# Two-operation wide factors with shifted phases, and seeds without a square root

## The chip, the cores and the metric

The kernel runs on one core of a Trainium2 chip. The metric is device time in microseconds of one execution; the kernel is one launch. Its engines run side by side, each with its own queue in program order: TensorE (PE, matmuls), VectorE (DVE), ScalarE (ACT, activation functions from loaded tables), GpSimd (POOL) and SyncE (SP, here only issuing transfers). They wait for each other with semaphores. PSUM is the memory that matmuls write to; SBUF is the large on-chip memory.

## The reference

A block with adaptive normalization around an S4 convolution, and a bilinear GLU. Shapes: u is 1x2048x640, the state has 192 entries for each of 640 channels, the GLU is 640 to 1536 and back, the modulation vector c has 640.

```python
mod = (silu(c) @ w_mod).reshape(1, 6, 1, 640)        # sa, ca, ga, sb, cb, gb
h = layernorm(x) * (1 + ca) + sa
x = x + ga * S4(h)
h = layernorm(x) * (1 + cb) + sb
x = x + gb * ((h @ w_gate) * (h @ w_up)) @ w_down

# S4: dt = exp(log_dt); A, B, C complex, 640 x 192
P = exp((dt * A)[:, :, None] * l)                    # l = 0 .. 2047
K = einsum("dn,dnl,dn->dl", C, P, dt * B).real       # the filter, 640 x 2048
y = irfft(rfft(pad(u)) * rfft(pad(K)))[:2048] + u * Dskip
```

## The kernel before, in words

The time falls into three parts: the startup and the filter with its Fourier transforms (to about 445 us), the rest of the convolution (to 546), and the GLU (to the end).

**The filter.** The sum over 192 states for 2048 positions is made as matmuls of two factors. A position is split into a low and a high part; for each of 40 blocks (n = 0 to 39, `NK`; eight for each of 5 groups, `db`, of 128 channels) the kernel builds four factor tiles: PtA and QtA (16 of 24 rows of the states), PtB and QtB (the other 8). P has 32 columns a row, Q, the wide factor, has 64. Each is a magnitude times a cosine and a sine. POOL makes the magnitudes EQ (128x1536) and EP (128x768) and the phases Ph (128x1536, 32-bit integers, where a whole turn is the whole range of the integer) by `outer` (L802) out of small tables: `tab_ph` (L785 to L787) makes LH from DL, and `tab_eq` (L796, L797) makes LQ from RL. ACT turns Ph into sines and cosines (`trig`, tiles tra and trb in PSUM, two buffers). DVE multiplies both (`qmul`, L857 to L859, for QtA and QtB; L864 for PtA, L884 for PtB), and PE multiplies the factors (L899, L914) into kg. EQ and EP have two buffers each, Ph two, QtA one.

**The seeds.** What a channel group starts from is made once per group by `u_seeds(db)`: from A, B, C and dt come rho (log magnitude), f (the frequency), and x and y, the real and imaginary part of B times C. From x and y the kernel needs a real amplitude and a phase: before, the modulus by two squares, an add and a square root, then the ratio of y to modulus and |x| added up, by a reciprocal and clipped to one, whose arctangent gives half the angle, psi; the amplitude is the modulus with x's sign. `trans` moves a 128x192 tile into the row order of the factors by matmuls against permutations (three matmuls a tile). RL and RH are multiples of rho (L681, L683), of which exponentials give RL, RH and LP. Each step is a letter, and the strings `SEG0` (first group) and `SEG` (groups 1 to 4) say which letters are issued together; a table of due times, which the change leaves alone, sets where a group of letters goes between the blocks. Seed 0 belongs to the startup; seeds 1 to 4 come at about 62 to 111, 157 to 197, 252 to 287 and 337 to 368 us. The scratch of these steps lies in three PSUM banks (psfa, psfb, psfc).

**The startup.** `mod_i` makes silu(c) into `sil` on ACT; `modrow` (L455) multiplies it with the six parts of w_mod, which are loaded through two tiles, t_tw and t_ti, one part after another; `u_fold` (L474 to L488) turns the rows into columns `mcol` and folds them into the factors' scale. The startup loop issues seed 0's letters and puts POOL's first tables between them at given positions (`P_PH`, `P_EP`, `P_MOD`).

**Order.** Every engine's order is the order in which the code issues the work. The loop over t (three steps per block) issues ACT's trig of a block, the seeds' and transforms' units that are due, DVE's products, POOL's tables for the next block and PE's matmuls. The names `ab`, `f16`, `gh`, `TV`, `Kta` in the rows are the Fourier transforms' and the normalization's tiles.

Of the kernel before, what the change touches and what calls it, by code (L numbers as in the profile page):

```python
# [18 lines left out]
P = 128  # L19
# [295 lines left out]
def tile_kernel(ctx: ExitStack, tc: tile.TileContext, I, out):  # L315
# [87 lines left out]
    V.memset(dskt, 0.0)  # L403
    xa = ring(f16, [P, 5, D], "f16")
# [179 lines left out]
    LP = [pk1.tile([P, 96, 8], F32, name=f"LP{i}") for i in range(3)]  # L584
    LH = pk1.tile([P, 192, 8], I32, name="LH")
    for t in LP:
        V.memset(t[:, :, 0:1], 1.0)
    RH = [pk1.tile([P, 11, 96], F32, name=f"RH{i}") for i in range(3)]
    RL = [pk1.tile([P, 4, 96], F32, name=f"RL{i}") for i in range(2)]
# [5 lines left out]
    def u_seeds(db):  # L595
# [7 lines left out]
        rho, f, amp = prm[:, 0, :], prm[:, 1, :], prm[:, 0, :]  # L603
        x, u, y, v = tb_[:, 0, :], tb_[:, 1, :], ta[:, 1, :], ta[:, 1, :]
# [3 lines left out]
        Rh, Rl, Dh, Dl, Lp = ([R[(2 * db + h) % len(R)] for h in range(2)] for R in (RH, RL, DH, DL, LP))  # L608
        g4 = lambda t: t.rearrange("p k (s r) -> p k s r", r=24)
# [7 lines left out]
        def trans(src, o):  # L617
            PE.matmul(o[:, :, 0:16], src[:, 0:128], perm[:, 0:128], start=True, stop=True)
            PE.matmul(o[0:64, :, 16:24], src[:, 128:192], perm[:, 128:192], start=True, stop=True)
            PE.matmul(o[64:128, :, 16:24], src[:, 128:192], perm[:, 192:256], start=True, stop=True)  # L620
# [32 lines left out]
        def s_c():  # L653
            ps = bank("ps").rearrange("p c (s r) -> p c s r", r=24)
            T["ps"] = ps
            trans(rho, ps[:, 0])
            trans(f, ps[:, 1])
            q = bank("q")
            act(u, x, AF.Square)
            act(q[:, 0], y, AF.Square)  # L660

        def s_d(h):
# [11 lines left out]
            if h:  # L674
# [3 lines left out]
        def s_r(h):  # L678
            ps = T["ps"]
            free(h, "ep", "eq", "lq")  # L680
            V.tensor_tensor(g4(Rl[h])[:, 0:3], ps[:, 0, hs[h]].unsqueeze(1).to_broadcast([P, 3, 4, 24]),  # L681
                            mults[:, 11:14].unsqueeze(2).unsqueeze(3).to_broadcast([P, 3, 4, 24]), op=OP.mult)
# [3 lines left out]
        def s_u():  # L686
            V.tensor_tensor(u, u, T["q"][:, 0], op=OP.add)
# [1076 lines left out]
```

## Time and profile before

| | |
|---|---|
| median of 3 runs | 995.83 us (995.24 to 996.85) |
| profiled execution, own time | 1000.16 us |
| its span in the profile | 998.3 us |
| mean granted TensorE clock | 0.955 |
| PE / DVE / ACT / POOL busy | 889.1 / 770.0 / 581.0 / 574.7 us |
| table loads on ACT | 24, 30.8 us in all |

A row of the timeline says when an instruction starts, how long it lasts, the engine, the line of the kernel, the operation, the tile written and the tiles read, the shape, how many such instructions the row stands for, and in brackets how long the engine was idle before it and which instruction released it. L320 is the helper of all activations on ACT. Rows of the chain of waits have a start, a length and what the time was spent on.

### The profile page before, as it was taken

Reading aid. Unit: us, or ns where it says so; the run is one execution under the profiler, and the core shown is the slowest. Engines: PE = TensorE matmul, PEld = TensorE weight load, DVE = VectorE, ACT = ScalarE, POOL = GpSimd, SP = SyncE. Lnnn points to the kernel's source line nnn. Section 1 sums busy time; section 2 is a strip of 40 time slices with the busy share of each in tenths; the row PEclk is TensorE's granted clock in tenths of the full one; section 3 lists DMA queues with packets and bytes.
Section 4 is the critical chain, followed back from the end, with each engine's and each line's share of the span. In section 5 each row is a group of like instructions: output and inputs, shape, how many; then the busy total and the mean of one; then the engine's idle time right before and its main releaser. Section 6 shows DMA issues by size and latency. Waiting matters only on the chain.

```text
span 998.3 us, 26784 instructions
## 1 busy us (share of the span) xinstructions
PE 889.1 (89%) x11190; PEld 728.2 (73%) x11190; DVE 770.0 (77%) x1391; ACT 581.0 (58%) x1055; POOL 574.7 (58%) x424
## 2 busy tenths in 40 slices
PE   4874699799889778997988999999999999999998
PEld 3653466576666466776766888879998888889998
DVE  8698568987989988795989877787576887768452
ACT  4759999987889797874574222235473422224331
POOL 4976899899869989960056667650112454442000
PEclk9867799899989989999999999999999999999999
DMA  7654665454545534559732542535635232212341
GB/s 243 239 145 155 217 237 163 159 165 135 154 131 161 171 108 149 161 152 305 221 113 59 188 169 69 184 132 159 211 133 202 96 98 80 79 53 63 96 159 53
DMA packets 141961, 148.96 MB, mean 149 GB/s; under 512 B 8976, under 2 KB 120080, under 8 KB 140432
## 3 DMA queue, kind: packets, MB, share of 16 engines
q1 hardware_dynamic: 140688, 146.33, 46.3%
q8 instruction: 88, 1.44, 0.6%
q10 hardware_dynamic: 1152, 0.92, 0.3%
q14 instruction: 33, 0.27, 0.1%
HBM read 108.36 MB, written 38.86 MB: 147 GB/s over the span
## 4 chain that ended last, share of the span: by engine, by line
PE 59%; ACT 14%; DVE 13%; issue 6%; POOL 5%; DMA 2%; DVEq 0%; SPq 0%; ACTq 0%; POOLq 0%
PE pa L1182 26%; PE pa L1597 16%; ACT tra L320 2%; ACT L320 2%; PE psfc L981 1%; ACT trb L320 1%; PE kg L899 1%; PE psfb L981 1%; PE psfa L1041 1%; PE kg L914 1%; POOL EQ L802 1%; PE psfb L1041 1%; PE psfa L981 1%; PE psfc L936 1%; POOL Pha L802 1%
## 5 line engine op out<-in xcount | busy, mean ns | idle before, releaser
L802 POOL TENSOR_TENSOR EQ<-LQ,RH 128x1536 f32<-128x1536 f32 x40 | 124.2, 3105 | 21.9 <-DVE QtB L859 21.7
L320 ACT ACTIVATE z<-pa 128x512 f32<-128x512 f32 x24 | 14.4, 599 | 166.4 <-PE pa L1182 115.4
L1146 DVE TENSOR_TENSOR wsgl<-wga,wsgh 128x640 fp32r<-128x640 f32 x72 | 68.2, 950 | 46.7 <-ACT wsgh L320 46.7
L320 ACT ACTIVATE wsgh<-wga 128x640 fp32r<-128x640 f32 x72 | 52.6, 732 | 71.2 <-PE pa L1597 39.8
L1546 POOL TENSOR_TENSOR z<-z,s 128x512 f32<-128x512 f32 x24 | 33.5, 1395 | 98.6 <-DVE s L1545 98.6
L1597 PE MATMUL pa<-wsgh,sh 128*128 128x384 f32 (+1 forms) x304 | 69.6, 310 | 0.0
L1597 PE MATMUL pa<-wsgl,sh 128*128 128x384 f32 (+1 forms) x304 | 69.3, 309 | 0.0
L1597 PE MATMUL pa<-wsgh,sl 128*128 128x384 f32 (+1 forms) x304 | 69.2, 309 | 0.0
L802 POOL TENSOR_TENSOR EP<-LP,RH 128x768 f32<-128x768 f32 x40 | 66.1, 1653 | 0.0
L1158 POOL TENSOR_TENSOR tf<-wur,wgb 128x256 f32<-128x256 f32 x24 | 19.2, 801 | 80.9 <-DVE wtl L1146 54.7
L802 POOL TENSOR_TENSOR Pha<-LH,DH 128x1536 int32<-128x1536 int32 (+1 forms) x21 | 62.5, 2974 | 3.0 <-ACT trb L320 2.6
L802 POOL TENSOR_TENSOR Phb<-LH,DH 128x1536 int32<-128x1536 int32 x20 | 62.3, 3117 | 2.9 <-ACT tra L320 2.9
L1146 DVE TENSOR_TENSOR wtl<-tf,wth 128x256 fp32r<-128x256 f32 (+1 forms) x72 | 60.0, 859 | 0.0
L914 PE MATMUL kg<-QtB,PtB 64*32 64x64 f32 x2560 | 47.9, 226 | 8.4 <-DVE QtB L858 8.4
L914 PEld LDWEIGHTS kg<-QtB,PtB 64*32 64x32 f32 x2560 | 40.9, 113 | 16.0 <-DVE QtB L858 9.5
L1544 DVE TENSOR_TENSOR s<-pa,s 128x512 f32<-128x512 f32 x24 | 16.6, 691 | 45.2 <-PE pa L1182 40.1
L1182 PE MATMUL pa<-sl,wth 128*128 128x512 f32 x144 | 45.2, 395 | 2.1 <-DVE sl L1146 2.1
L1597 PEld LDWEIGHTS pa<-wsgh,sl 128*128 128x128 f32 x304 | 46.6, 188 | 0.0
L1597 PEld LDWEIGHTS pa<-wsgl,sh 128*128 128x128 f32 x304 | 46.6, 188 | 0.0
L1597 PEld LDWEIGHTS pa<-wsgh,sh 128*128 128x128 f32 x304 | 46.5, 188 | 0.0
L1182 PE MATMUL pa<-sh,wth 128*128 128x512 f32 x144 | 45.1, 395 | 1.1 <-ACT sh L320 1.1
L1182 PE MATMUL pa<-sh,wtl 128*128 128x512 f32 x144 | 45.4, 397 | 0.0
(608 smaller groups left out, 2957.3 us busy)
## 6 DMA issues: line engine op xcount, KB each, us to landing
wga<-wdg SPq DMA_DIRECT2D x24, 640.0 KB, 4.0
wga<-B_w_gate SPq DMA_DIRECT2D x12, 640.0 KB, 5.7
wgb<-B_w_gate SPq DMA_DIRECT2D x24, 320.0 KB, 3.4
wur<-B_w_up SPq DMA_DIRECT2D x24, 320.0 KB, 4.0
xb<-x2d SPq DMA_DIRECT2D x6, 1280.0 KB, 7.4
TVb<-WD SPq DMA_DIRECT2D x22, 256.0 KB, 3.4
t_tw<-w_mod SPq DMA_DIRECT2D x3, 1600.0 KB, 7.8
t_ti<-w_mod SPq DMA_DIRECT2D x3, 1600.0 KB, 7.7
```

The lines of the kernel that those rows point to most:

```text
L320: return S.activation(o, i, f, **kw)
L802: G.tensor_tensor(o.rearrange("p x (h l) -> p x h l", l=8), lo.unsqueeze(2).to_broadcast([P, rows, nh, 8]), hi.rearrange("p h x -> p x h") ...
L899: PE.matmul(kg[j * 32 : j * 32 + 32, dd, :], PtA[:, c, dl * 4 + j, :], QtA[:, c, dl * 4 + j, :], start=dd == 0 and c == 0, stop=False, til ...
L914: PE.matmul(kg[j * 32 : j * 32 + 32, dd, :], PtB[lo : lo + 64, c, r, :], QtB[lo : lo + 64, c, r, :], start=False, stop=dd == 7 and c == 1, ...
L981: PE.matmul(r[c][par * 64 : par * 64 + 64, i, :], t_tw[:, k0 + k, c, :], src[:, k, :], start=True, stop=True, tile_position=(0, par * 64))
L1041: PE.matmul(r[par][:, i], w, v, start=c == 0, stop=c == 1, tile_position=(lo, 0))
L1146: V.tensor_tensor(lo, v, hi, op=OP.subtract)
L1158: G.tensor_tensor(t[:, 0:2], u[:, 0:2], g[:, 0:2], op=OP.subtract)
L1182: PE.matmul(ps, w[a][:, k], x[b][:, l], start=n == 0 and m == 0, stop=n == 2 and m == len(ks) - 1)
L1544: V.tensor_tensor(S67[i], ps, S6[i], op=OP.add)
L1546: G.tensor_tensor(ZT[i], ZT[i], S67[i], op=OP.add)
L1597: PE.matmul(ACC[tb][t][c], x[:, ts], w[:, cs], start=st, stop=f == NF - 1 and n == 2 and (c == 0 or t % 2 == 1))
```

## The change

Three things change together.

1. `qmul` makes a wide factor in two operations in place of three. The phases are put an eighth of a turn ahead (`eighth`, added where `tab_ph` copied DL into LH, and in psi), so that the sign that one third of a wide factor needed falls away; the two halves of the 64 columns then differ only in which of sine and cosine is read first.
2. The seeds have no Square, Abs and Sqrt. The step x makes q = x·y and its sign, prm = 2·(y, x)·sign, and adds and subtracts it; the step X takes reciprocal and quotient, clipped to one on both sides; f takes the arctangent, and a sine and a cosine of it; n adds a quarter turn by sign; m multiplies x and y with the cosine and sine, and G adds the two by accumulating both in the same matmul group. For groups 1 to 4, RL and RH of both halves come from one operation each (B), and so do the exponentials (E); LP, RH and RL are single tiles with the halves side by side.
3. In the startup a sine of a constant is issued first on ACT, the letters have a new order, and `mod_i` is issued with the first EP, at loop position 9, where it stood at position 1.

```diff
-SEG0 = ("l", "a", "b", "c", "ud", "r", "x", "e", "f", "G", "g", "D", "h", "v", "R", "")
-SEG = ("l", "a", "b", "c", "ud", "D", "r", "R", "x", "eE", "f", "g", "h", "v")
-P_PH, P_EP, P_MOD = 3, 6, 1
+SEG0 = ("l", "a", "b", "cx", "d", "X", "f", "nh", "vr", "e", "mG", "D", "", "", "R", "")
+SEG = ("l", "a", "b", "cx", "d", "D", "X", "B", "f", "E", "nm", "G", "h", "v")
+P_PH, P_PSI, P_EP = 3, 7, 9
...
-        def trans(src, o):
-            PE.matmul(o[:, :, 0:16], src[:, 0:128], perm[:, 0:128], start=True, stop=True)
...
+        def trans(o, *srcs):
+            for t, c, k in ((o[:, :, 0:16], slice(0, 128), 0), (o[0:64, :, 16:24], slice(128, 192), 128), (o[64:128, :, 16:24], slice(128, 192), 192)):
+                for i, src in enumerate(srcs):
+                    PE.matmul(t, src[:, c], perm[:, k : k + c.stop - c.start], start=i == 0, stop=i == len(srcs) - 1)
...
-            act(u, x, AF.Square)
-            act(q[:, 0], y, AF.Square)
+            bank("q")
...
-            act(u, u, AF.Sqrt)
-            act(pe[:, 0], x, AF.Abs)
-            V.tensor_scalar(pe[:, 1], x, 0.0, 0.5, op0=OP.is_ge, op1=OP.subtract)
...
+            q = T["q"][:, 0]
+            V.tensor_tensor(q, x, y, op=OP.mult)
+            V.tensor_scalar(sgn, q, 0.0, 0.5, op0=OP.is_ge, op1=OP.subtract)
+            V.scalar_tensor_tensor(prm, tb_[:, 1::-1, :], 2.0, sgn.unsqueeze(1).to_broadcast([P, 2, N]), op0=OP.mult, op1=OP.mult)
+            V.tensor_tensor(x, x, prm[:, 0, :], op=OP.add)
+            V.tensor_tensor(y, y, prm[:, 1, :], op=OP.subtract)
+
+        def s_X():
+            q = T["q"][:, 0]
+            V.reciprocal(q, x)
+            V.tensor_scalar(q, q, 3e38, -3e38, op0=OP.min, op1=OP.max)
+            V.tensor_tensor(q, y, q, op=OP.mult)
+            V.tensor_scalar(arg, q, 1.0, -1.0, op0=OP.min, op1=OP.max)
 
         def s_f():
-            pe = T["pe"]
+            T["pe"] = pe = bank("pe")
+            act(arg, arg, AF.Arctan)
+            act(pe[:, 1], arg, AF.Sin)
+            act(pe[:, 0], arg, AF.Sin, scale=-1.0, bias=halfpi)
+
+        def s_n():
+            V.scalar_tensor_tensor(arg, sgn, 0.5 * math.pi, arg, op0=OP.mult, op1=OP.add)
+
+        def s_m():
...
+            V.scalar_tensor_tensor(xy, xy, dt2[:, db : db + 1], T["pe"], op0=OP.mult, op1=OP.mult)
...
-        G.tensor_copy(lh[..., 0:1], one(d[0]))
-        G.tensor_tensor(lh[..., 1:2], one(d[0]), one(d[1]), op=OP.add)
...
+            G.tensor_tensor(lh[..., 0], d[0], eighth[:, a : a + 1].unsqueeze(2).to_broadcast([P, 4, 24]), op=OP.add)
+        G.tensor_tensor(lh[..., 1:2], lh[..., 0:1], one(d[1]), op=OP.add)
...
-        return [lambda: V.tensor_tensor(Qt[:, :, :, 0:32], tr[:, :, :, ::-1], e[:, :, 0:32].unsqueeze(1).to_broadcast([P, 2, R, 32]), op=OP.mult),
-                lambda: V.tensor_tensor(Qt[:, 0, :, 32:64], tr[:, 0], e[:, :, 32:64], op=OP.mult),
-                lambda: V.scalar_tensor_tensor(Qt[:, 1, :, 32:64], tr[:, 1], -1.0, e[:, :, 32:64], op0=OP.mult, op1=OP.mult)]
+        return [lambda h=h: V.tensor_tensor(Qt[:, :, :, 32 * h : 32 * h + 32], tr[:, ::-1] if h else tr[:, :, :, ::-1],
+                                            e[:, :, 32 * h : 32 * h + 32].unsqueeze(1).to_broadcast([P, 2, R, 32]), op=OP.mult) for h in range(2)]
...
+    act(colT[:, 0:1], halfpi, AF.Sin)
     exp_acc(dt, ldt)
...
-        elif i == P_EP:
+        elif i == P_PSI:
+            tab_ph(0, 0)
+            mk_ph(0, 0)
+        elif i == P_EP:
+            mod_i()
             mk_ep(0)
-        elif i == P_MOD:
-            mod_i()
-    tab_eq(0)
-    tab_ph(0, 0)
-    mk_ph(0, 0)
-    mk_eq(0)
+            tab_eq(0)
+            mk_eq(0)
```

What this does to the order of the instructions is seen at two places. The first is ACT's queue in the startup, where `sil` is the operand of the modulation matmuls, tra the transposed amplitude and LP, RH, RL the exponentials of half 0. Before:

```order
L320 ACTIVATE psfb<-ptb 128x2x192
L320 ACT_TABLE_LOAD
L320 ACTIVATE sil<-ccol 128x5
L320 ACTIVATE ptb<-ptb 128x192
L320 ACTIVATE psfa<-pta 128x192
L320 ACT_TABLE_LOAD
L320 ACTIVATE ptb<-ptb 128x192
L320 ACTIVATE psfb<-ptb 128x192
L320 ACT_TABLE_LOAD
L320 ACTIVATE LP_147<-RL_157 128x96 x7
```

Now:

```order
L320 ACTIVATE psfb<-ptb 128x2x192
L320 ACTIVATE pta<-pta 128x192
L320 ACTIVATE psfb<-pta 128x192
L320 ACTIVATE psfb<-pta,halfpi 128x192
L320 ACT_TABLE_LOAD
L320 ACTIVATE LP<-RL 128x96 x7
L320 ACTIVATE RH<-RH 128x1056
L320 ACTIVATE RL<-RL 128x288
L320 ACTIVATE RL<-tra 128x2x96
L320 ACT_TABLE_LOAD
L320 ACTIVATE sil<-ccol 128x5
```

The Silu has moved behind the arctangent, the exponentials and the copy of the amplitude. The second place is DVE's queue in seed 4, with the factors of the blocks around it. Before:

```order
L864 TENSOR_TENSOR PtAa<-tra,EP_144 128x1024
L884 TENSOR_TENSOR PtB<-trb,EP_144 128x512
L857 TENSOR_TENSOR QtB<-trb,EQ_142 128x16x32
L858 TENSOR_TENSOR QtB<-trb,EQ_142 128x8x32
L859 SCALAR_TENSOR_TENSOR QtB<-trb,EQ_142 128x8x32
L687 TENSOR_TENSOR ptb<-ptb,psfc 128x192
L667 CAST psfc<-psfa 128x192
```

Now (ptb, pta and prm are in SBUF, psfc in PSUM):

```order
L882 TENSOR_TENSOR PtAa<-tra,EP_147 128x1024
L703 TENSOR_TENSOR psfc<-ptb 128x192
L704 TENSOR_SCALAR pta<-psfc 128x192
L705 SCALAR_TENSOR_TENSOR prm<-ptb,pta 128x384
L706 TENSOR_TENSOR ptb<-ptb,prm 128x192
L707 TENSOR_TENSOR ptb<-ptb,prm 128x192
L902 TENSOR_TENSOR PtB<-trb,EP_147 128x512
L876 TENSOR_TENSOR QtB<-trb,EQ_145 128x16x32 x2
L679 CAST psfc<-psfa 128x192
```

The five operations of x now stand between the factors PtA and PtB of one block, where one add stood behind QtB. The chain that made the quotient, ten rows further down before, is the step X, and stands ahead of the joint RL and RH.

More of the change, by code (lines that the diff above doesn't have):

```diff
@@ L655, in s_c @@
             T["ps"] = ps
[L656 to L660 removed]
+            trans(ps[:, 0], rho)
+            trans(ps[:, 1], f)
+            bank("q")
         def s_d(h):
```

108 lines of the change are left out of this document (53 added, 55 removed).

## The prediction

> **What bounds the kernel now.** I read the stage windows first, then POOL's waits, then the chain of waits, and last the timeline of single engines where the chain changes hands. The windows show each engine's busy time by stage (us, busy PE, PEld, DVE, ACT, POOL, granted clock, DMA share, GB/s):
>
> ```profile
> 118.00:445.00 327.00, 284.11 (x6656) 211.70 (x6652) 277.83 (x464) 282.70 (x502) 298.61 (x174) 0.95 0.51 158
> ...
> 546.00:998.00 452.00, 445.19 (x2372) 394.67 (x2372) 312.70 (x504) 157.11 (x304) 164.16 (x151) 1.00 0.38 125
> ```
>
> From 546 us PE is busy 445.2 of 452 us, and nothing of the change lies there: what is lost or won earlier passes through to the end. From 118 to 445 us POOL is busiest (298.6 of 327, 28.4 us idle), with ACT and DVE 16 and 21 us behind it. Two of POOL's waits in the whole run (total, times, longest):
>
> ```profile
> POOL EQ L802 <- DVE QtB L859: 21.7, 7, 7.1
> ...
> POOL DL L742 <- issue: 9.7, 2, 8.1
> ```
>
> So POOL stops where DVE has not yet freed an EQ buffer, or where a seed's psi (made by L737 on DVE, used by L742) is late. A delay of DVE between two blocks is a delay of POOL once the two EQ buffers are used up. The chain of waits (start, length) before that stage is not POOL:
>
> ```profile
> 18.77 4.57 PE psfb L455 x10
> ...
> 27.05 6.77 DMA t_tw<-w_mod
> ...
> 39.57 1.03 PE kg L899 x64
> ```
>
> The modulation rows (L455) run first, the tile t_tw is loaded again behind them, and the first block's matmuls (L899) stand behind that in PE's queue.
>
> **The wide factors.** One block's QtA, start by start on DVE:
>
> ```profile
> 82.93 1.23 DVE L857 TENSOR_TENSOR QtA<-trb,EQ 128x1024 f32<-128x1024 f32 x1 [0.53 <-issue]
> 84.07 0.68 DVE L858 TENSOR_TENSOR QtA<-trb,EQ 128x512 f32<-128x512 f32 x1
> 84.67 0.68 DVE L859 SCALAR_TENSOR_TENSOR QtA<-trb,EQ 128x512 f32<-128x512 f32 x1
> 85.27 0.34 DVE L687 TENSOR_TENSOR ptb<-ptb,psfb 128x192 f32<-128x192 f32 x1
> ```
>
> 1.14 + 0.60 + 0.60 = 2.34 us become two of 1.14, 2.28 us. By the same step QtB saves as much at most, so 0.12 us a block, 4.8 us of DVE over 40 blocks, in a stage where DVE has 49 us of idle time. I count it only beside seed 4, with 0.4. The eighth of a turn costs POOL one add for a copy in a table, 0.1 us for each of ten tables; I set it to nothing.
>
> **Startup.** Before, the Silu that the modulation rows need is out early; ACT now does it last, behind the arctangent, the exponentials and the copy of G's result into RL:
>
> ```profile
> 8.03 0.21 ACT L320 ACTIVATE sil<-ccol 128x5 f32<-128x5 f32 x1
> 12.17 1.25 DVE L683 TENSOR_TENSOR RH<-psfc,mults 128x1056 f32<-128x1056 f32 x1
> 17.02 0.87 DVE L565 BATCH_NORM_STATS2 st<-f16a 128x6 f32<-128x320 f32 x2
> 20.87 0.35 DVE L737 TENSOR_SCALAR ptb<-tra 128x192 int32<-128x192 f32 x1
> 7.62 0.80 PE L618 MATMUL psfc<-ct,prm 128*128 128x128 f32 x2
> 8.52 0.32 PE L620 MATMUL psfc<-ct,prm 128*64 128x64 f32 x1
> ```
>
> A transposed source takes PE 8.84 − 7.62 = 1.2 us. In the new order DVE has x (about 1.75 us: four operations of 192 elements at 0.34 like L687 above and one of 384 at some 0.5, less what they overlap), the steps of half 0, X and n before psi; I estimate psi at 18.6 instead of 20.87. RL and RH (to 20.3) and the statistics (to 21.2) follow, then m, done at 21.8. PE's G has two sources, 2.4 us, to 24.2; the copy ends at 24.6, a table load takes 1.28 (the row of seed 1 below), and the Silu ends at about 26.3. The first L455 starts at 26.4 instead of 18.77: +7.6, and t_tw's reload, L899 and the fold of the rows (L474) behind it move along. QtA of block 2, which on DVE stands behind the fold's mcol steps, moves as far. I take **+7.6 us**. Bounds: +9 if n is also held up, +3 if the later mcol steps meet an idle POOL, which would give back up to 4 us (next rows).
>
> **The lock on two SBUF inputs.** The kernel before hardly has DVE operations with both inputs in SBUF while POOL works; the seeds' scratch is in PSUM. The few that there are stand here:
>
> ```profile
> 51.02 0.17 DVE L480 TENSOR_TENSOR mcol<-mcol 128x5 f32<-128x5 f32 x1
> 52.68 3.01 DVE L482 TENSOR_TENSOR mcol<-mcol 128x5 f32<-128x5 f32 x1
> 55.95 0.16 DVE L484 TENSOR_TENSOR mcol<-psfb,mcol 128x5 f32<-128x5 f32 x1
> 52.58 3.09 POOL L802 TENSOR_TENSOR EQ<-LQ,RH 128x1536 f32<-128x1536 f32 x1
> ```
>
> The same five elements take 0.17 us or 3.01, and the long one ends at 55.69, where POOL's EQ ends (55.67); L484, with one input in PSUM, takes 0.16 while POOL is busy. In the change, x has four such operations and n one. The Trainium skill, page "SBUF — State Buffer", section "Who interferes with whom", says it as a rule: a DVE instruction with two SBUF inputs and a GpSimd instruction that reads SBUF exclude each other for a whole instruction, and one with at most one SBUF input does not contend; by that rule all five are exposed, and the trace's 3.01 against 0.16 us agrees. For SCALAR_TENSOR_TENSOR with two such inputs no row stands beside a running POOL: between 0.55 us (free) and a POOL operation of 3.1; I take the second, the nearest row being L482. Between two held operations POOL gets its next one in, so x costs about four POOL operations.
>
> **Seed 1.** POOL is idle beside it, so no lock, and ACT has the say:
>
> ```profile
> 82.48 3.10 POOL L802 TENSOR_TENSOR EQ<-LQ,RH 128x1536 f32<-128x1536 f32 x1 [7.07 <-DVE QtB L859]
> 97.83 1.28 ACT L320 ACT_TABLE_LOAD   x1
> 111.71 0.60 ACT L320 ACTIVATE trb<-Pha 128x512 f32<-128x512 int32 x1
> ```
>
> The group of table loads in the whole run is
>
> ```profile
> L320 ACT ACT_TABLE_LOAD x24 | 30.8, 1283 | 4.6 <-DMA pta<-A_A_re 4.2
> ```
>
> In the 13.9 us from 97.83 to 111.71 two of four loads go (2.6 us), Sqrt and Abs go (0.6), two sines come (0.6), and the joint exponentials save what the fixed part of nine operations costs, about 0.8 by my reading of the pitches; less the wait of the new sines for their operand that makes 11.1, −2.8. DVE's x, 1.75 us longer than the add it replaces, delays the normalization's operands by some 0.6 on the same chain. **−2.2 us**, between −2.5 and +1.
>
> **Seeds 2 to 4** lie where POOL works without a pause. For each I take first what the change costs without a lock, then the lock. The rows:
>
> ```profile
> 159.17 3.11 POOL L802 TENSOR_TENSOR Pha<-LH,DH 128x1536 int32<-128x1536 int32 x1
> 159.32 0.34 DVE L687 TENSOR_TENSOR ptb<-ptb,psfc 128x192 f32<-128x192 f32 x1
> 192.46 3.10 POOL L802 TENSOR_TENSOR EQ<-LQ,RH 128x1536 f32<-128x1536 f32 x1 [4.67 <-DVE QtB L859]
> 258.15 3.11 POOL L802 TENSOR_TENSOR Pha<-LH,DH 128x1536 int32<-128x1536 int32 x1
> 285.30 0.35 DVE L737 TENSOR_SCALAR ptb<-psfa 128x192 int32<-128x192 f32 x1
> 341.73 3.10 POOL L802 TENSOR_TENSOR EQ<-LQ,RH 128x1536 f32<-128x1536 f32 x1
> 344.79 1.64 POOL L802 TENSOR_TENSOR EP<-LP,RH 128x768 f32<-128x768 f32 x1
> 346.40 3.10 POOL L802 TENSOR_TENSOR Pha<-LH,DH 128x1536 int32<-128x1536 int32 x1
> 359.69 0.60 ACT L320 ACTIVATE trb<-Pha 128x512 f32<-128x512 int32 x1
> ```
>
> *Seed 2.* Without a lock nothing: X and the joint RL and RH only change places with work behind them before the stall at 192.46. With it, x meets Pha until 162.22 and three short POOL operations (0.36, 0.40, 0.76 us), and ends at 165.5 instead of 161.3: **+4.1**, between 0 and +9.
>
> *Seed 3.* Without a lock DVE has 1.0 us more between 258 and psi (x, X, n and m 5.1 against 4.1 for the add, the compare and the chain L706 to L711), and G's two sources on PE, which psi waits for, 1.1 more: +2.1. With it, x meets Pha to 261.2, EQ, and EP, and ends at 267.3 instead of 261.1, +6.2. POOL waits at L742, the 8.1 us above, for exactly this chain, so **+8.3**, between +2 and +11.
>
> *Seed 4.* x stands behind PtAa, at 340.96. Without a lock X (2.4 us) and the joint RL and RH (2.9 instead of 3.1) push the exponentials, which trb at 359.69 stands behind on ACT, by 3.1. With it x meets Phb's end at 341.73, then EQ, EP and Pha in turn, and ends at 350.6 instead of 342.9: +7.7; less 0.4 for the factors, **+10.4**, between +3 and +12.
>
> What these hide: the eight loads less (10.3 us of ACT) and the shorter exponentials lie mostly in seeds 2 to 4, where ACT has 44 us of idle time; they help only if ACT's order was what held DVE and so POOL.
>
> **Sum.** 7.6 − 2.2 + 4.1 + 8.3 + 10.4 = +28.2 us. The profiled execution had 1000.16 us with a span of 998.3; it becomes 1028.4. The median of the timed runs, 995.83, lies 4.3 lower, so 1024.0.
>
> **The rivals.** *No lock for these forms* (the four are 128x192 or 128x384, and no such pair is in the stage before): 7.6 − 2.2 + 0 + 2.1 + 3.1 = +10.6, 1006.4. For it: nothing but the lack of a row for them; against it: L482. *The lock costs a whole rotation everywhere*: x always meets the rest of an operation (1.4), two or three long ones and a wait of POOL for its own turn, 10 us for each of three seeds, 8.1 more than x alone, and DVE never regains it: 10.6 + 3 × 8.1 = +34.9, with n held up once more per seed up to +38, 1031 to 1034. *Faster*: the mechanism is ACT's order. If DVE frees EQ late because it waits for sines that stand on ACT behind a seed's work, then the 10.3 us of loads and 0.8 us of exponentials in each of five seeds shorten POOL's 21.7 us of waits at EQ. With half of these 14.3 us on the path, the startup lost in the 7.1 us that POOL waits before seed 1's EQ anyway, and the held x inside POOL's other waits, the time is 995.8 − 7.1 = 989. It decides once DVE waits for ACT longer than x is held; for it speaks that ACT is busy 282.7 of 327 us, against it that x stands ahead of the factors on DVE itself, so a held x delays them whatever ACT does. *No change*: the same, with the startup's 7.6 us not absorbed, 996.
>
> **How the numbers follow.** The lock as summed 0.55, no lock 0.23, the full rotation 0.10, faster 0.08, no change 0.04. The forecast is 1024.0. The range runs from 1003 (no lock, 1006.4, with the startup at the lower part of its bounds) to 1035 (the full rotation); below it lie the 12 in 100 of the last two, above a few. A measurement of this kernel cannot tell less than about 0.2%, 2 us, from no change: faster 0.08, same 0.04, slower 0.88.
>
> **What would show it.** In the changed kernel's profile: the Silu near 26 us and the first modulation matmul behind it; the x operations of seeds 2 to 4 (two inputs in SBUF) at 1 to 3 us each, ending where a POOL operation ends, and those of seed 1 at 0.35 to 0.55; 16 table loads; QtA in two rows 1.14 apart; psi of seed 3 some 18 us later than 285.3 (7.6 − 2.2 + 4.1 + 8.3). The forecast is wrong if x's operations are short beside a busy POOL, if the Silu's delay shrinks before block 2's QtA, or if POOL's idle time from 118 to 445 us falls below 28 us although x is held up.

## The result and the profile after

| | before | changed |
|---|---|---|
| median, runs of the same batch | 995.54 us (991.83 to 996.85, 4 runs) | 1043.36 us (1042.76 to 1044.27, 4 runs) |
| ratio to before, 95% interval | | 1.0464 [1.0424, 1.0505] |
| profiled execution, own time | 1000.16 us | 1043.4 us |
| its span | 998.3 us | 1041.6 us |
| mean granted TensorE clock | 0.955 | 0.941 |

The change costs 47.8 us. The forecast was 28.2 us more, and the time lies 8 us above the upper end of the range. The stage windows of the changed kernel (columns as in the prediction) say where it went:

```profile
126.00:491.00 365.00, 298.17 (x6662) 220.16 (x6658) 286.55 (x399) 277.01 (x466) 301.19 (x174) 0.89 0.46 141
491.00:592.00 101.00, 89.08 (x1193) 67.17 (x1186) 88.42 (x188) 57.70 (x103) 28.54 (x30) 1.00 0.61 183
592.00:1041.00 449.00, 442.54 (x2362) 392.44 (x2360) 310.12 (x499) 155.68 (x300) 161.48 (x148) 1.00 0.38 124
```

The last two stages are as long as before (101 and about 450 us). The filter stage has grown from 327 to 365 us with hardly more work in it: POOL is busy 2.6 us longer, DVE 8.7 us longer, ACT 5.7 us less. The difference is waiting: POOL is idle 63.8 of the 365 us, where it was idle 28.4 of 327. PE's granted clock fell from 0.95 to 0.89 there. What POOL waited for, over the whole run (total, times, longest, us):

```profile
POOL EQ L821 <- DVE QtB L876: 44.3, 9, 9.9
...
POOL Pha L821 <- ACT trb L320: 11.2, 5, 6.1
POOL Phb L821 <- ACT tra L320: 11.1, 7, 3.2
```

The wait for DVE to free an EQ buffer has doubled, from 21.7 to 44.3 us. Of DVE's own waits ahead of QtA, the one that has grown most is for PE: 12.4 us for kg (L917), where it was 2.1 in the kernel before. And PE, in the same stage, waits for this:

```profile
PE kg L932 <- DVE QtB L876: 17.2, 5, 9.5
PE psfa L999 <- DVE RH L698: 11.4, 2, 10.3
PE psfc L978 <- DVE pta L714: 10.3, 1, 10.3
...
PE psfc L999 <- DVE pta L714: 7.7, 1, 7.7
...
PE psfb L458 <- DVE pta L714: 3.6, 1, 3.6
```

Three rows name L714, the last operation of the step X, and its operand's PSUM bank. L978 and L999 are matmuls of the Fourier transforms and L458 is a modulation row: none of them uses anything that X computes. They write the bank that X used as scratch. In the kernel before, that bank was free earlier; the same transform matmul of seed 2 waited only 0.19 us, for the shifts D (L675):

```profile
163.29 0.44 PE L981 MATMUL psfc<-ghb,t_tw 128*64 128x128 f32 x4 [0.19 <-DVE ptb L675]
```

Seed 2 of the changed kernel, in three rows of DVE (L703 is the first operation of x), two of POOL and two of PE, each group with the start times that tie them together:

```profile
170.71 2.01 DVE L703 TENSOR_TENSOR psfc<-ptb 128x192 f32<-128x192 f32 x1
...
183.77 0.36 DVE L714 TENSOR_SCALAR pta<-psfc 128x192 f32<-128x192 f32 x1
188.92 2.36 DVE L876 TENSOR_TENSOR QtA<-trb,EQ 128x1024 f32<-128x1024 f32 x2 [4.79 <-PE kg L917]
```

```profile
169.39 3.11 POOL L821 TENSOR_TENSOR Pha<-LH,DH 128x1536 int32<-128x1536 int32 x1
...
215.23 3.10 POOL L821 TENSOR_TENSOR EQ<-LQ,RH 128x1536 f32<-128x1536 f32 x1 [9.85 <-DVE QtB L876]
```

```profile
184.18 0.70 PE L999 MATMUL psfc<-ghb,t_tw 128*64 128x128 f32 x4 [7.72 <-DVE pta L714]
...
187.65 1.10 PE L917 MATMUL kg<-QtA,PtAb 128*32 128x64 f32 x64
```

Two things happen one behind the other. x is held on DVE: its first operation takes 2.01 us instead of 0.37 and ends at 172.72, where POOL's Pha ends (172.50). Then the bank that x wrote at 170.71 stays taken until X's last clip has read it, at 184.1, because x and X are now two steps with the shifts and three factor tiles between them. PE stands at L999 for 7.72 us. kg of the current block, which needs nothing from the bank, is behind L999 in PE's queue and starts at 187.65; QtA, which has one buffer, waits 4.79 us for kg; and QtB, which frees POOL's EQ buffers, follows QtA on DVE. POOL's EQ at 215.23 is the same block's as the one at 192.46 before: 22.8 us later, and behind an idle time of 9.85 us where there were 4.67. DVE's own queue splits the loss: from the QtA ahead of x (168.44, before 156.99) to the next one (188.92, before 167.67) it grows by 9.8 us, of which 4.1 are x, 0.9 is X in the place where RL and RH of half 0 stood, and 4.8 the wait for kg.

The shift of each block against the profiled execution of before, read from the start of QtA, shows how the loss grows:

| stretch (blocks) | forecast | measured |
|---|---|---|
| startup (to 3) | +7.6 | +6.3 |
| seed 1 (3 to 10) | −2.2 | +3.6 |
| seed 2 (10 to 17) | +4.1 | +13.2 |
| seed 3 (17 to 27) | +8.3 | +9.1 |
| seed 4 (27 to 39) | +10.4 | +13.9 |

### The profile page after: what moved, and what is told of

It reads as the page before. It is cut to its first block, busy times and chain, and to the rows that moved or that the text cites. A ratio compares the mean times of both kernels' runs of the same rounds, so it can differ in the third digit from the quotient of the medians.

```text
span 1041.6 us, 26715 instructions
## 1 busy us (share of the span) xinstructions
PE 901.3 (87%) x11220; PEld 734.1 (70%) x11220; DVE 780.9 (75%) x1314; ACT 568.0 (55%) x1001; POOL 578.4 (56%) x424
## 5 line engine op out<-in xcount | busy, mean ns | idle before, releaser
L821 POOL TENSOR_TENSOR EQ<-LQ,RH 128x1536 f32<-128x1536 f32 x40 | 124.2, 3105 | 44.5 <-DVE QtB L876 44.3
L821 POOL TENSOR_TENSOR Pha<-LH,DH 128x1536 int32<-128x1536 int32 (+1 forms) x21 | 62.7, 2988 | 11.6 <-ACT trb L320 11.2
L876 DVE TENSOR_TENSOR QtA<-trb,EQ 128x1024 f32<-128x1024 f32 x40 | 47.0, 1217 | 26.7 <-ACT trb L320 13.8
L932 PE MATMUL kg<-QtB,PtB 64*32 64x64 f32 x2560 | 51.2, 236 | 17.5 <-DVE QtB L876 17.2
L876 DVE TENSOR_TENSOR QtA<-tra,EQ 128x1024 f32<-128x1024 f32 x40 | 47.0, 1216 | 21.2 <-PE kg L917 7.1
L932 PEld LDWEIGHTS kg<-QtB,PtB 64*32 64x32 f32 x2560 | 43.7, 119 | 26.4 <-DVE QtB L876 19.4
```

Of the source, the lines that this page charges most:

```text
L821: G.tensor_tensor(o.rearrange("p x (h l) -> p x h l", l=8), lo.unsqueeze(2).to_broadcast([P, rows, nh, 8]), hi.rearrange("p h x -> p x h") ...
L876: return [lambda h=h: V.tensor_tensor(Qt[:, :, :, 32 * h : 32 * h + 32], tr[:, ::-1] if h else tr[:, :, :, ::-1], e[:, :, 32 * h : 32 * h ...
L932: PE.matmul(kg[j * 32 : j * 32 + 32, dd, :], PtB[lo : lo + 64, c, r, :], QtB[lo : lo + 64, c, r, :], start=False, stop=dd == 7 and c == 1, ...
```

## The experiments

All were run in three rounds beside the kernel before; "+9 us" is the median less that of before in the same batch. The shifts of the blocks, by the same reading as above, are put together here:

| kernel | to block 3 | seed 1 | seed 2 | seed 3 | seed 4 |
|---|---|---|---|---|---|
| changed | 6.3 | +3.6 | +13.2 | +9.1 | +13.9 |
| old14 | 7.4 | −1.8 | +2.0 | −0.4 | −1.6 |
| new14 | −5.8 | +1.2 | +11.8 | +9.4 | +15.5 |
| x_psum | 6.7 | +5.6 | +12.7 | +9.4 | +6.0 |
| x_bank | 6.5 | +0.3 | +6.0 | +5.0 | +16.7 |
| x_both | 7.3 | +0.7 | +4.7 | +4.2 | +11.2 |
| no_X | 4.7 | −0.1 | +4.6 | +3.7 | +6.0 |
| hold | −1.9 | +0.4 | +4.3 | +5.0 | 0.0 |
| lock4 | −1.7 | +6.7 | +5.6 | +9.7 | +9.1 |
| ctrl4 | −1.9 | +0.8 | +1.1 | +3.6 | +1.5 |

The first column shows −1.7 to −5.8 for kernels whose startup is that of before; why is told in the last section.

### Which part of the change

**factors_only**: the kernel before with the two-operation factors and the shifted phases.

```diff
-        return [lambda: V.tensor_tensor(Qt[:, :, :, 0:32], tr[:, :, :, ::-1], ...
-                lambda: V.tensor_tensor(Qt[:, 0, :, 32:64], tr[:, 0], ...
-                lambda: V.scalar_tensor_tensor(Qt[:, 1, :, 32:64], tr[:, 1], -1.0, ...
+        return [lambda h=h: V.tensor_tensor(Qt[:, :, :, 32 * h : 32 * h + 32], ...
```

> The kernel before with only the two-operation factors and the phases an eighth of a turn ahead; the seeds and the startup stay as they were. If the factors are off the path, as the prediction counts them, the time is 991 to 996 us. If the loss of 48 us has any part in the factors (for instance POOL's added add, or DVE reaching waits earlier), the time is above 998.

**seeds_only**: the changed kernel with the three-operation factors and unshifted phases.

```diff
-        return [lambda h=h: V.tensor_tensor(Qt[:, :, :, 32 * h : 32 * h + 32], ...
+        return [lambda: V.tensor_tensor(Qt[:, :, :, 0:32], tr[:, :, :, ::-1], ...
...
-        V.memset(eighth[:, k : k + 1], k * 2**29)
+        V.memset(eighth[:, k : k + 1], 0)
```

> The changed kernel with the factors made in three operations again and the phases not shifted (the added POOL add stays and adds zero). If the loss lies in the seeds and the startup alone, the time is 1043 to 1049 us; if the factors take part in it, below 1040.

Measured: factors_only 994.86 us, ratio 0.9983 [0.9956, 1.001]; seeds_only 1043.98 us, 1.0501 [1.0464, 1.0538]. The factors are off the path, and the whole loss is with the seeds and the startup.

**old14** keeps the changed startup, seed 0 and factors, and takes the old code for seeds 1 to 4; **new14** is its mirror, with the old startup and seed 0 and the new seeds 1 to 4.

```diff
-            at(T0["q"][db - 1], u_seeds, db)
+            at(T0["q"][db - 1], u_seeds_old, db)
```

> The changed kernel with the seeds of the kernel before for channel groups 1 to 4; startup, seed 0 and factors as changed. If the startup's 6.4 us (block 2's QtA, changed less before) pass through to the end, 1002 to 1005 us; if later waits absorb them, 995 to 999.

```diff
-gp0 = u_seeds(0)
+gp0 = u_seeds_old(0)
...
-SEG0 = ("l", "a", "b", "cx", "d", "X", "f", "nh", "vr", "e", "mG", "D", "", "", "R", "")
+SEGO = ("l", "a", "b", "c", "ud", "r", "x", "e", "f", "G", "g", "D", "h", "v", "R", "")
```

> The reverse: the startup and seed 0 of the kernel before, the changed seeds for groups 1 to 4, the factors as changed. If the parts add up, 1043.4 less what old14 shows of the startup: 1036 to 1039. If the startup's delay only shifts where the seeds' delays fall, 1040 to 1044.

Measured: old14 1004.14 us (+10.0), 1.0096 [1.0064, 1.0127]; new14 1029.89 us (+35.8), 1.0377 [1.0307, 1.0447]. 10 and 36 add up to 46 of the 47.8 us, so the two parts can be studied apart, though new14 came out 6 us below the range expected of it. The forecast had 7.6 for the first and 20.6 for the second: the missing time is in seeds 1 to 4.

### Two suspects in the seeds, mended one at a time

**x_psum** makes x in eight operations, each with at most one input in SBUF, with the bank's two halves as scratch (q and r).

```diff
-            q = T["q"][:, 0]
-            V.tensor_tensor(q, x, y, op=OP.mult)
+            q, r = T["q"][:, 0], T["q"][:, 1]
+            V.tensor_copy(r, x)
+            V.tensor_tensor(q, r, y, op=OP.mult)
...
-            V.scalar_tensor_tensor(prm, tb_[:, 1::-1, :], 2.0, ...
-            V.tensor_tensor(x, x, prm[:, 0, :], op=OP.add)
-            V.tensor_tensor(y, y, prm[:, 1, :], op=OP.subtract)
+            V.tensor_scalar(q, q, 0.0, 0.5, op0=OP.is_ge, op1=OP.subtract)
+            V.scalar_tensor_tensor(r, x, 2.0, q, op0=OP.mult, op1=OP.mult)
+            V.scalar_tensor_tensor(q, y, 2.0, q, op0=OP.mult, op1=OP.mult)
+            V.tensor_tensor(x, x, q, op=OP.add)
+            V.tensor_tensor(y, y, r, op=OP.subtract)
```

> The changed kernel with step x rebuilt from eight operations, each with at most one input in SBUF (x is first copied into PSUM), so that POOL cannot hold them; about 0.9 us more DVE work per seed. Theory of the lock: the four held operations cost 2.6, 2.5 and 4.2 us of DVE in seeds 2 to 4 by the trace, 9.3 in all, so 1034 us, down to 1026 if POOL's own hold-up and the order behind it come on top. Rival, the scratch bank: PE waits for the bank that X reads and not for x, so the time falls by no more than 4 us, 1039 to 1044.

**x_bank** leaves x as it is and gives X, in groups 1 to 4, a part of another bank, which the seed holds anyway.

```diff
         def s_X():
-            q = T["q"][:, 0]
+            q = T["ps"][:, 1].rearrange("p s r -> p (s r)") if db else T["q"][:, 0]
```

> The changed kernel with X's scratch, in seeds 1 to 4, in the second half of the bank that holds the transposed f (free by then) and not in bank q, so that q is free after the shifts, as before. Theory of the bank: PE's waits on L714 (3.6, 10.3 and 7.7 us in seeds 1, 3 and 2) shrink to those on the last shift, some 5.5 us in seed 2 and 4.7 in seed 3, 1030 to 1036 us. Theory of the lock: x is held as before, the time stays at 1041 to 1044.

**x_both** is the two edits together.

> x_psum and x_bank in one kernel. If lock and bank are two separate costs, their savings of about 6 and 11 us add up: 1026 to 1028 us. If they meet on one chain (x stands ahead of the shifts that free the bank), the savings overlap or the one makes the other worth more: x held short lets the bank go 4 to 5 us earlier in seeds 2 and 3, so 1018 to 1025.

Measured: x_psum 1037.63 us, 1.0425 [1.0386, 1.0464]; x_bank 1032.71 us, 1.0378 [1.0344, 1.0413]; x_both 1024.53 us, 1.0259 [1.0211, 1.0307]. The lock's mend gives back about 4 us (its interval overlaps that of the changed kernel), the bank's about 9, and both about 20. By the medians that is more than the sum; the intervals of the ratios are too wide to insist on it, and in the profiles the shift to block 39 falls by 6, 12 and 18 us, which adds up. The lock's mend is worth less than the holds that it takes away because its eight operations take DVE 2.8 us in each seed, where x unheld takes 2.0.

The first group of DVE's operations in x_psum (busy us, mean ns) shows that no hold is left, and PE's waits show that the bank is taken as before:

```profile
L704 DVE TENSOR_TENSOR psfc<-psfc,ptb 128x192 f32<-128x192 f32 x3 | 1.1, 365 | 0.1
```

```profile
PE psfc L981 <- DVE pta L717: 8.5, 1, 8.5
PE psfc L1002 <- DVE pta L717: 8.5, 1, 8.5
```

(L717 is X's clip in this kernel.) So seeds 2 and 3 stay where they were, +12.7 and +9.4, and only seed 4, where the holds were longest, falls, from 13.9 to 6.0. In x_bank it is the other way round: seeds 2 and 3 fall to 6.0 and 5.0, and seed 4 does not, at 16.7. PE's waits for X are gone there, and what is late next stands in their place, the shifts behind the held x:

```profile
PE psfc L978 <- DVE DH L683: 5.6, 1, 5.6
...
PE psfc L999 <- DVE DH L683: 4.7, 1, 4.7
```

In x_both these two are 3.8 and 3.1 us: x is on DVE ahead of the shifts, even if nothing holds it.

### The suspects put into the kernel before, one at a time

A mend shows what is left once the next cost takes over. So the two suspects, and the plain length of x, were also added to the kernel before, each alone.

**hold** copies one column of the bank onto itself ahead of RL of half 0, in seeds 1 to 4: the bank stays taken, with 0.15 us of work.

```diff
             free(h, "ep", "eq", "lq")
+            if db and h == 0:
+                V.tensor_copy(T["q"][:, 0, 0:1], T["q"][:, 0, 0:1])
```

> The kernel before, with one copy of a single column of bank q onto itself ahead of RL of half 0 in seeds 1 to 4 (0.2 us of DVE each, no result is touched), so that the bank is let go only there. If a bank held past the shifts stops PE, with QtA's matmuls behind it in PE's queue, the time rises by 3 to 10 us: 997 to 1005 against 994. If not, it stays within 2 us.

**lock4** adds four operations of 192 elements with both inputs in SBUF behind the step u, whose result nobody reads; **ctrl4** adds the same four with one input in PSUM.

```diff
+            if db:
+                for _ in range(4):
+                    V.tensor_tensor(f, x, u, op=OP.mult)
```

> The kernel before, with four added DVE operations behind u in seeds 1 to 4, each of 128x192 with both inputs in SBUF; what they write is read by nobody. The control is ctrl4. If POOL holds such operations, each waits for a POOL operation where POOL is busy, and lock4 lies 6 to 20 us above ctrl4; if DVE has slack for it, both agree within 3 us.

```diff
+            if db:
+                for _ in range(4):
+                    V.tensor_tensor(f, x, T["q"][:, 0], op=OP.mult)
```

> The same as lock4 with one of the two inputs in PSUM (bank q), so the same 1.1 to 1.4 us of DVE per seed without the lock. If DVE's length alone costs what no_X showed (some 6 us for 2.1 us in each seed), 997 to 1000 us; if it is hidden, 993 to 996.

Measured, with before at 997.36 us in this batch: hold 1007.34 us, 1.0112 [1.0071, 1.0153]; lock4 1027.73 us, 1.0273 [1.0212, 1.0335]; ctrl4 1003.58 us, 1.0052 [1.002, 1.0085].

*The bank* alone is worth 1.1%, 11 us by the ratio. It shows as the same kind of wait (L682 is the copy):

```profile
PE psfc L983 <- DVE psfc L682: 3.3, 1, 3.3
PE psfc L962 <- DVE psfc L682: 3.1, 1, 3.1
...
PE psfb L455 <- DVE psfb L682: 1.6, 1, 1.6
```

The waits sum to 8 us here and to 21.6 in the changed kernel, where x and X are longer and later. So the bank may well cost more than 11 us there; x_bank, which takes it away, shows 9.

*The lock.* The sixteen added operations of lock4, and then the sixteen of ctrl4:

```profile
L690 DVE TENSOR_TENSOR prm<-ptb 128x192 f32<-128x192 f32 x16 | 25.0, 1565 | 0.8
```

```profile
L690 DVE TENSOR_TENSOR prm<-ptb,psfc 128x192 f32<-128x192 f32 x12 | 4.2, 351 | 0.3
L690 DVE TENSOR_TENSOR prm<-ptb,psfb 128x192 f32<-128x192 f32 x4 | 1.4, 351 | 0.1
```

1565 against 351 ns for the same operation, by where the second input lies. lock4 spends 25.0 − 5.6 = 19.4 us more on DVE and is 2.2% slower than ctrl4, 22 us: in this place a microsecond on DVE is about a microsecond at the end. ctrl4 says the same without a lock: 5.6 us of DVE, 5 us of time. The Trainium skill, page "SBUF — State Buffer", section "Who interferes with whom", has the rule that a DVE instruction with two SBUF inputs contends with a GpSimd instruction that reads SBUF, and that one with at most one SBUF input does not, outside DVE's two-port modes; these two kernels agree with it, with 1565 and 351 ns. The prediction gave the rule without that last condition.

### The startup

**silu_only** is the changed kernel with the Silu issued early, at the loop position where it stood before.

```diff
-P_PH, P_PSI, P_EP = 3, 7, 9
+P_MOD, P_PH, P_PSI, P_EP = 1, 3, 7, 9
...
-        elif i == P_EP:
+        elif i == P_MOD:
             mod_i()
+        elif i == P_EP:
```

> The changed kernel with the Silu issued early on ACT, as before, and nothing else. The prediction's startup step says the Silu sets the first modulation row: then 7 us come back, 1036 to 1037. Rival: in PE's queue the row also stands behind G's matmuls, which end at 24.07 us where the Silu ends at 25.97; then only 1.9 us come back, 1041 to 1042.

**silu_row** also issues the first modulation row ahead of G's matmuls, in another bank.

```diff
-((-88999, -86998), (-89000, -87998))),
+((-88999, -86998), (-93000, -87998))),
-    psf="abcabbabcacbacba...
+    psf="abcababacbcabcab...
```

> silu_only, and the first modulation row moved ahead of G in PE's queue (with its PSUM bank changed so that it is free there). If the order in PE's queue is the rest of the startup's cost, the row starts near 18.7 us as before, G some 1 us later than now, the reload of t_tw 5 us earlier, and 5 us come back in all: 1037 to 1039. If the startup's delay is absorbed later (POOL waits near 82 us in any case), the time stays at 1041 to 1044.

Measured: silu_only 1041.14 us, 1.0436 [1.0395, 1.0477]; silu_row 1040.44 us, 1.0438 [1.0387, 1.0489]. Neither is told apart from the changed kernel. PE's timeline says why; first the changed kernel, then silu_only, then silu_row (L628 with ptb is G's matmuls):

```profile
22.21 1.86 PE L628 MATMUL tra<-ct,ptb 128*128 128x128 f32 x12 [3.50 <-DVE ptb L728]
26.02 4.58 PE L458 MATMUL psfb<-t_tw,sil 128*128 128x256 f32 x10 [1.96 <-ACT sil L320]
```

```profile
23.42 1.86 PE L628 MATMUL tra<-ct,ptb 128*128 128x128 f32 x12 [3.50 <-DVE ptb L728]
25.21 4.58 PE L458 MATMUL psfb<-t_tw,sil 128*128 128x256 f32 x10
```

```profile
25.98 4.61 PE L458 MATMUL psfa<-t_tw,sil 128*128 128x256 f32 x10 [5.97 <-issue]
30.38 1.70 PE L628 MATMUL tra<-ct,ptb 128*128 128x128 f32 x12
```

The Silu is what the row waits for in the changed kernel, as forecast, but it is late by 1.96 us only. With the Silu early, the row waits for G ahead of it in PE's queue, and G is itself 1.2 us later, as the early Silu costs ACT two table loads more, one of them between the arctangent and the sine, where the changed kernel has none. With the row ahead of G, its bank (psfa) is still read by seed 0's shifts, the last of which ends at 25.88, and the row starts at 25.98 all the same. The startup's loss is thus not the Silu's place but seed 0's longer chain, which the queue, the tables and the banks each pass on.

**start2** tries that on x_both: Silu early, a dummy sine behind it, and n and m right behind the sines.

```diff
-SEG0 = ("l", "a", "b", "cx", "d", "X", "f", "nh", "vr", "e", "mG", "D", "", "", "R", "")
+SEG0 = ("l", "a", "b", "cx", "d", "X", "f", "nmh", "vr", "e", "G", "D", "", "", "R", "")
...
+            mod_i()
+            act(colT[:, 0:1], halfpi, AF.Sin)
```

> Built on x_both. In the startup the Silu is issued early with a sine of a constant behind it (so the table is back before the arctangent), and n and m stand right behind the sines on DVE, ahead of psi, RL, RH and the statistics. If m's place on DVE, with G and the modulation rows behind it in PE's queue, is what made the startup late, the first modulation row starts at 20 to 21 us instead of 26, and 5 us come back from x_both's 1024.5: 1018 to 1021. If the startup's delay is lost in later waits anyway, 1023 to 1026.

Measured: 1020.69 us, 1.0236 [1.0157, 1.0315], not told apart from x_both. The first row does start at 22.96 instead of 26.02, but the first block's kg still comes at 47.28 (46.19 in the changed kernel), since later rows then wait for the reloads of their tiles:

```profile
22.96 4.36 PE L458 MATMUL psfb<-t_tw,sil 128*128 128x256 f32 x10
...
31.97 2.40 PE L458 MATMUL psfb<-t_ti,sil 128*128 128x256 f32 x10 [1.43 <-DMA t_ti<-w_mod]
...
40.04 5.16 PE L458 MATMUL psfa<-t_tw,sil 128*128 128x384 f32 x10 [2.44 <-DMA t_tw<-w_mod]
```

### What is left

**all3** is x_both with silu_row.

> x_psum, x_bank and silu_row in one kernel. If the three account for the loss, what is left above the kernel before (997 us in these runs) is the joint and later RL, RH and exponentials of seed 4 and the longer chain of seeds: 1012 to 1022 us. If something else carries the loss, 1025 or more.

**x_late** is x_both with x behind the shifts D.

```diff
-SEG = ("l", "a", "b", "cx", "d", "D", "X", "B", "f", "E", "nm", "G", "h", "v")
+SEG = ("l", "a", "b", "c", "d", "Dx", "X", "B", "f", "E", "nm", "G", "h", "v")
```

> Built on x_both. In seeds 1 to 4 step x stands behind the shifts of both halves and not ahead of them and of PtB and QtB. If x's place ahead of a block's factors and ahead of the shifts that free bank q is part of what is left (x_both still shows PE waiting 3.1 and 3.8 us for L683), 3 to 8 us come back: 1017 to 1022. If only the length of DVE's work counts, wherever it stands, the time stays at 1023 to 1026.

**no_X** is x_both with X's four operations replaced by one clip; it leaves the quotient out.

```diff
-            V.reciprocal(q, x)
-            V.tensor_scalar(q, q, 3e38, -3e38, op0=OP.min, op1=OP.max)
-            V.tensor_tensor(q, y, q, op=OP.mult)
-            V.tensor_scalar(arg, q, 1.0, -1.0, op0=OP.min, op1=OP.max)
+            V.tensor_scalar(arg, x, 1.0, -1.0, op0=OP.min, op1=OP.max)
```

> Built on x_both, with X's reciprocal, clip, product and clip left out and one clip of x in their place, so the angle is not the reference's; 2.1 us less DVE work in each seed. If the length of DVE's seed work is what is left, 6 to 9 us come back, 1015 to 1018; if DVE's length has slack in these stages, less than 3 us, 1021 to 1026.

**best** is x_both with start2 and x_late.

> start2 and x_late together on x_both. If the two are separate costs, 1011 to 1016 us; the kernel before lies near 997 in these runs, and nothing here is expected to fall below it.

**best_split** is best with RL and RH, and the exponentials, in two operations each, one for each half, as before.

```diff
-SEG = ("l", "a", "b", "c", "d", "Dx", "X", "B", "f", "E", "nm", "G", "h", "v")
+SEG = ("l", "a", "b", "c", "d", "Dx", "rX", "R", "f", "eE", "nm", "G", "h", "v")
...
-E=one(s_e, 0, 1)
+E=one(s_e, 1)
```

> Built on best (start2 and x_late), with RL and RH and the exponentials of the two halves separate again, half 0's ahead of X. If the joint operations are part of the 20 us that are left, because the bank of the transposed rho is let go later and half 0's exponentials wait for half 1's operands, 3 to 6 us come back from 1016.6: 1010 to 1014. If only DVE's length is left, 1016 to 1019.

| kernel | median, us | ratio, 95% |
|---|---|---|
| x_both, for comparison | 1024.53 | 1.0259 [1.0211, 1.0307] |
| all3 | 1024.26 | 1.0257 [1.0195, 1.0319] |
| x_late | 1023.18 | 1.027 [1.0234, 1.0306] |
| no_X | 1017.95 | 1.0213 [1.0173, 1.0252] |
| best | 1016.63 | 1.021 [1.0173, 1.0246] |
| best_split | 1018.81 | 1.0264 [1.0201, 1.0328] |

x_late and all3 change nothing that can be told. no_X gives back some 5 us by the ratio, for about 2.1 us less DVE in each of five seeds, though its interval overlaps that of x_both: it fits ctrl4, that the length of the seeds' work on DVE shows at the end. The joint operations are no cause that shows: best_split is not faster than best. No version beat the kernel before; best, the fastest that keeps the new seeds, is 2.1% slower.

## Why the prediction was wrong

**The direction and the mechanism of the lock: right.** Where POOL works beside them, x's operations take 2.01 (seed 2), 2.91 (seed 3), and 0.97, 1.42 and 3.14 us (seed 4), and the SCALAR_TENSOR_TENSOR form, of which no row had been there, is held too, 1.42 us in seed 4 against 0.56 unheld. Seed 3's first operation and then seed 4 on DVE, and POOL beside seed 4:

```profile
281.92 2.91 DVE L703 TENSOR_TENSOR psfc<-ptb 128x192 f32<-128x192 f32 x1 [0.34 <-ACT hfc L320]
...
376.93 1.42 DVE L705 SCALAR_TENSOR_TENSOR prm<-ptb,pta 128x384 f32<-128x384 f32 x1
378.38 3.14 DVE L706 TENSOR_TENSOR ptb<-ptb,prm 128x192 f32<-128x192 f32 x1
381.44 0.35 DVE L707 TENSOR_TENSOR ptb<-ptb,prm 128x192 f32<-128x192 f32 x1
```

```profile
376.17 1.76 POOL L821 TENSOR_TENSOR EP<-LP,RH 128x768 f32<-128x768 f32 x1
377.89 3.42 POOL L821 TENSOR_TENSOR Pha<-LH,DH 128x1536 int32<-128x1536 int32 x1
383.73 3.09 POOL L821 TENSOR_TENSOR EQ<-LQ,RH 128x1536 f32<-128x1536 f32 x1 [2.43 <-DVE QtB L876]
```

**The size of the lock: too large.** The step "x costs about four POOL operations" gave holds of 4.2, 6.2 and 7.7 us, 18 in all. Measured, from the durations in each seed less the free ones (0.37, 0.56, 0.36, 0.35), they are 2.6, 2.5 and 4.2 us, 9.3 in all. The step took POOL to have its next operation ready each time. In seeds 3 and 4 it does not: POOL lives on the EQ buffers that DVE frees, so while DVE is held POOL runs dry (idle from 381.31 to 383.73 above, and for 3.88 us in seed 3), and the rest of x runs free. In seed 2 POOL had its short table operations next, and behind Pha they held x by only another 0.9 us.

**The scratch bank in seeds 1 to 3: the failed step.** The prediction costed what x and X cost DVE, and said of seed 2, "Without a lock nothing: X and the joint RL and RH only change places with work behind them". What it never asked is who waits for the scratch of x and X. The bank is part of a ring that the transforms' matmuls use; its lifetime, which ended with the shifts, now lasts until X's last operation. That wait is on PE, in three rows of 21.6 us in all (seeds 1, 3 and 2), and kg, QtA, QtB and EQ stand behind it. Taken away, it gives back 9 us (x_bank); added alone to the kernel before it costs 11 (hold). Seeds 1 to 4 cost 36 us (new14) where the four terms sum to 20.6. Seed 3's total, +9.1 for a forecast of +8.3, is luck: its holds were 2.5 us and not 6.2, x_bank takes 4.1 us off it, and POOL's wait at the line of L742, which the forecast saw growing, was 7.4 us after 8.1.

**Seed 4: the sum too small for another reason.** No wait for X's bank stands there. Its +13.9 has 1.5 us at block 28, 6.4 at block 29 (4.2 of holds, the rest x's own length and a wait of 0.8 for its scratch bank), 2.8 at block 30, where QtA waits for the sines behind the exponentials, as the forecast's 3.1 said, and 3.2 at block 31, for which it had no term: there POOL's wait at LQ, for the amplitude's copy into RL, has grown from 3.36 to 6.63 us. The rows before, and then now:

```profile
361.11 1.23 DVE L857 TENSOR_TENSOR QtA<-trb,EQ 128x1024 f32<-128x1024 f32 x1 [1.50 <-ACT trb L320]
...
365.25 0.36 POOL L796 COPY LQ<-RL 128x96 f32<-128x96 f32 x1 [3.36 <-DVE RL L736]
```

```profile
404.01 2.35 DVE L876 TENSOR_TENSOR QtA<-trb,EQ 128x1024 f32<-128x1024 f32 x2 [5.09 <-ACT trb L320]
...
409.61 0.35 POOL L815 COPY LQ<-RL 128x96 f32<-128x96 f32 x1 [6.63 <-DVE RL L751]
```

**DVE's plain length: too small.** The terms without a lock were 0, 2.1 and 3.1 us for seeds 2, 3 and 4. ctrl4 shows 5 us for 1.4 us more in each of four seeds, and no_X about as much, less surely, for 2.1 us less: DVE's work ahead of the factors is on the path. The sign that the prediction gave for seed 3, psi some 18 us later than 285.30, came out as 30.8 (316.10).

**Seed 1: wrong sign.** It was to gain 2.2 us and lost 3.6. x was indeed free there (0.37 us a row), but the stretch from its start to block 10 has the PE wait of 3.6 us for X's bank (psfb, L458), and with X's bank elsewhere the loss is 0.3 (x_bank). The gain was also put too high: the joint exponentials take 5.00 us on ACT where the two halves took 5.14, which saves 0.14 us and not 0.8.

**The startup: about right.** Forecast +7.6; by the profiles 6.3, by timing 10.0 (old14, whose interval is 6 to 13 us). The Silu (25.76 us, forecast 26.3) and the first modulation row (26.02, forecast 26.4) came where they were put. That the Silu's place is the cause was half right: G is only 1.96 us ahead of it.

**The factors and the loads: right.** QtA stands in two rows of 1.2 us, off the path; there are 16 table loads; what the 10.3 us less of them gained, no run separates:

```profile
L320 ACT ACT_TABLE_LOAD x16 | 20.5, 1283 | 2.9 <-issue 2.6
```

**The rivals.** The full rotation (1031 to 1034) came nearest in time, for a reason that did not happen: the holds were shorter than forecast, not longer. The two errors, too large a lock and no bank, partly hid each other.

**What adds up, and what stays open.** Startup 10; the lock 9.3 us of holds, at the 1.1 us that lock4 shows for each, about 10; the bank 9 to 11; the added length 5 to 10, by ctrl4 and no_X. That is an estimate of 34 to 41 of 47.8 us. The rest stays open; that it lies where these meet is likely, since hold's waits are shorter than those of the changed kernel, but not shown. Of best's remaining 20 us the profiles put some 15 into seeds 1 to 4 and 2.4 ahead of block 3, measured from a profile of before that is itself 4.3 us above the median; which operation would have to move to win them was not found.

## What to carry to other kernels

When a step is split, lengthened or moved, list its buffers as well as its instructions: for each, who writes the same slot next, on which engine, and what stands behind that writer in its queue. An operand that can lie in PSUM should, if a DVE operation would else read two from SBUF beside a busy POOL. Where several costs stand on one chain, add each alone to the old kernel too; mending them one by one in the new one shows only what the next one leaves free.

## What the hardware showed beside this

**POOL's operations stretch a little too.** While DVE's held operations ran in seed 4, POOL's EP took 1.76 and its Pha 3.42 us (rows above), against 1.64 and 3.10 elsewhere in the same run.

**The same chain can cost 2.75 or 7.2 us.** The fold's mcol steps are the same eleven small DVE operations in all kernels, from the first mcol to block 2's QtA. In the profiled execution of before they take from 50.20 to 57.43 us, with the 3.01 us hold that the prediction quotes. In factors_only, which has the same eleven operations, they meet POOL's short table operations, and take 2.75 us:

```profile
49.10 0.17 DVE L481 TENSOR_SCALAR mcol<-psfb 128x5 f32<-128x5 f32 x1 [3.74 <-PE psfb L477]
...
50.20 0.57 DVE L485 TENSOR_TENSOR mcol<-mcol 128x5 f32<-128x5 f32 x1
...
51.85 2.34 DVE L864 TENSOR_TENSOR QtA<-trb,EQ 128x1024 f32<-128x1024 f32 x2
```

new14, the other kernel with the old startup and the new phases, takes 2.85 us; hold, lock4 and ctrl4 take 6.3 to 6.7. That, with a chain that starts 0.9 to 1.4 us earlier than in the profile of before, is the negative first column of the table of shifts. It fits the profiled execution of before being 4.3 us above its median, but each kernel has one kept profile, so whether executions of one kernel differ in this way is not shown. The chain also has a hold that the count of inputs in SBUF does not cover: its second TENSOR_SCALAR from SBUF to SBUF, with one input, took 1.43 us in the kernel before and 0.17 in factors_only.

**PE's granted clock is low around its long waits.** Behind the 7.72 us wait at L999 the same groups of four matmuls take 0.64 to 0.70 us, and 0.39 to 0.44 in the kernel before. The granted clock of 170 to 190 us in the changed kernel was 0.66, and of 160 to 180 in the kernel before 1.00:

```profile
170.00:190.00 20.00, 11.59 (x217) 10.30 (x218) 14.93 (x27) 8.43 (x14) 17.40 (x10) 0.66 0.42 133
```

```profile
160.00:180.00 20.00, 17.00 (x482) 13.28 (x482) 18.95 (x35) 18.62 (x32) 19.76 (x12) 1.00 0.66 206
```

Not all of that follows from the long wait: the clock was 0.50 from 172 to 176 us already, ahead of it. The 10.3 us wait of seed 3 is clearer. The clock was 1.00 until PE stopped at 286, 0.50 from 290 on, and still 0.50 for the matmuls from 296.5 to 302; kg, at 300.31, took 1.93 us where it takes 1.10 at full clock. There a wait of PE cost its length and then some of the work behind it.
